# Attention inside a fused kernel: per-row maxima turned by VectorE instead of TensorE

## The chip, the cores and the metric

The kernel runs on one core of a Trainium2 chip. The metric is the device time of one execution in microseconds, and the figure compared is the median of several executions. Engines are named as the profile names them: PE is TensorE, DVE is VectorE, ACT is ScalarE, POOL is GpSimd and SP is SyncE, which here only issues transfers.

## What is computed

The kernel runs a causal attention with a decay, then two mixture-like matrix stages on its output. The change lies in the attention alone:

```python
# q, k, v: (4, 8, 576, 64); f: (4, 8, 576)
scores = scale * np.matmul(q, k.transpose(0, 1, 3, 2))
cum = np.cumsum(np.log(np.clip(f, 0.0001, 1.0)), axis=-1)
scores = np.where(causal, -1000000000.0, scores + cum[:, :, :, None] - cum[:, :, None, :])
scores = scores - np.max(scores, axis=-1, keepdims=True)
attn = np.exp(scores)
attn = attn / (np.sum(attn, axis=-1, keepdims=True) + 1e-09)
out = np.matmul(attn, v)
# then: x = out as (2304, 512); x = ((x @ w1) * (x @ w2)) @ w3 @ w_out
# then: every row goes to one of 8 experts (512 -> 1024 relu -> 512) and is gated
```

## The kernel before, in words

The attention works on 16 units, one for each of 4 batches and 4 pairs of heads. A unit's scores are computed twice. The first time queries lie on the partitions, so that a maximum over the keys is a reduction along the free axis. The second time keys lie on the partitions, so that the weights come out in the layout that the product with `v` needs. Between the two the maxima have to change from a column (one number per partition) into a row, since the second pass adds them by a product with one row of a matrix.

The steps of unit n, by the names in the table `START` (L50):

- `X1`, `X3`, `X2` (`scores_of`, L229) and `XL` (`scores_last`, L248) are the products of the first pass on PE. `XL` holds the last 64 queries of both heads. Their results lie in three PSUM buffers (`pss`, L94), which the eight tiles of a unit use in turn: a product waits until the reader of the tile three places before it is done.
- `m0` to `m3` and `mL` (`maxima`, L257, L262) are the reductions on DVE. Each writes one column of the tile `M` of the unit: columns 0 to 7 are the four blocks of 128 queries for each head, column 8 is the last block for both heads.
- `Tm` (`turn`, L268) is a PE transpose of `M` into a free corner of a score tile in PSUM. For units 2 to 14 that is the tile of `X1` of the next unit. `tc` (`turned`, L273) is an ACT copy of nine rows from there to the tile `mt` in SBUF. `mv` (`spread_maxima`, L276, issued through `move`, L193) is two SP transfers from `mt` into rows 0 and 64 of the tile `MR`.
- `GA` to `GD` are the second pass on PE, `HA` to `HD` (`weights`, L281, with `last`) add decay and maxima to it from `CK` and `MR`, and `eA` to `eD` (L301) are the exponentials on ACT, which write the tile `PT`.
- `a0` to `a4` (L307) and `s1` to `s3` (L319) are the causal masks of `PT` and the sums over its blocks on POOL.
- `p0`, `p1`, `p3` (L328) are the products with `v` on PE. They and the sums `su` (L344) belong to the unit before the one whose `PT` is being made.
- `kh`, `qh` (ACT, L213) and `kl`, `ql` (DVE, L220) split the operands into a high and a low part. `lk`, `lq`, `lv` (L198) are the loads of k, q and v on SP, `ck` (L207) is the load of the decay rows into `CK`, `qd` (L193) copies the last queries into `QD`, `zs` (L355) stores the sums of the weights.
- `c0` to `c6` convert one piece of a later weight per unit: `c0` is its load on SP (L465), `c1` and `c5` are ACT (L472, L481), `c2`, `c3`, `c4` are DVE (L474, L476, L478), `c6` is POOL (L483). `xm` (L380) is a further POOL product in units 5, 7, 9 and 11.

The order is written out by hand. Every step has a time `START[x] + SHIFT[n, x] + PERIOD * n`, all steps of all units are sorted by it, and every engine executes its own in that order. The times set the order on an engine and nothing else; waits come from data and from buffers in use. After the attention, and already among its last units, PE multiplies the converted weight pieces (`AFTER`, L64), and the matrix stages follow.

Of the kernel before, what the change touches and what calls it, by code (L numbers as in the profile page):

```python
# [11 lines left out]
F32 = mybir.dt.float32  # L12
F32R = mybir.dt.float32r
# [4 lines left out]
ACTF = mybir.ActivationFunctionType  # L18
# [4 lines left out]
B, H, S, D = 4, 8, 576, 64  # L23
NP = H // 2
# [4 lines left out]
P = 128  # L29
# [18 lines left out]

PERIOD = 9.8
START = {  # L50
# [8 lines left out]
}  # L59
SHIFT = {(0, "ck"): 8.38, (1, "ck"): 8.38, (2, "ck"): 8.38, (3, "ck"): 8.38, (0, "qd"): -2.0, (0, "lq"): 7.41, (0, "lk"): 14.91, (1, "lk"): 15.41, (2, "lk"): 14.9, (3, "lk"): 5.8, (4, "lk"): 2.1, (2, "lq"): 0.5, (0, "kh"): 5.05,  (1, "lq"): 0.5, (0, "XL"): -4.55, (0, "mL"): -5.9, (0, "Tm"): -1.8, (0, "tc"): -1.8, (0, "mv"): -2.6, (1, "Tm"): -0.1, (1, "tc"): -0.1}  # L60

FILL = {(0, "XL"): 10, (1, "X0"): 1, (0, "HA"): 1, (0, "HB"): 3, (1, "XL"): 3, (2, "X0"): 2}

# [13 lines left out]
def attention(nc, tc, ident, xT, rz, xs, wc, q, k, v, f):  # L77
# [6 lines left out]
    V, A, G, PE, SP = nc.vector, nc.scalar, nc.gpsimd, nc.tensor, nc.sync  # L84
    with (
# [31 lines left out]
        MRs = [p1.tile([P, S], F32R, name=f"MR{i}") for i in range(2)]  # L117
# [3 lines left out]
        Ms = [p1.tile([P, 64], F32, name=f"M{i}") for i in range(2)]  # L121
# [58 lines left out]
        st = {}  # L180

        def tl(s, key, shape, dt=F32, bufs=2):
            if key in ("kh", "kl"):
                ring = KHs[key == "kl"]
                s[key] = ring[s["n"] % len(ring)]
                return s[key][:, :S]
            if key not in s:
                pool = p2 if key in ("qr", "kr", "kh", "kl", "qh", "ql") else p3
                s[key] = pool.tile([P, *shape], dt, name=f"{key}_{s['n']}", tag=key, bufs=bufs)
            return s[key]  # L190

        def move(out, src):
            SP.dma_start(out=out.bitcast(F32), in_=src.bitcast(F32))  # L193
# [71 lines left out]
                    accum_out=Ms[s["n"] % 2][:, c:c + 1],  # L265
                )

        def turn(s):  # L268
            x = st[s["n"] + 1]["x", 1][:, 256:] if 1 < s["n"] < B * NP - 1 else s["x", 4][:, 896:]
            s["t"] = x[0:64, :P]  # L270
            PE.transpose(s["t"], Ms[s["n"] % 2], ident)

        def turned(s):  # L273
            A.activation(out=tl(s, "mt", (P,), F32R)[0:9], in_=s["t"][0:9], func=ACTF.Copy)

        def spread_maxima(s):  # L276
            t, MR = s["mt"], MRs[s["n"] % 2]
            move(MR[0:P:64, 0:512].rearrange("h (i c) -> h i c", c=P), t[0:8])
            move(MR[0:P:64, 512:S], t[8:9])

        def weights(s, g, last):  # L281

# [91 lines left out]
        def first_tile(s, x):  # L374
# [5 lines left out]
                    G.tensor_tensor(out=xT[:, i, 0:512], in0=xT[:, i, 0:512], in1=d, op=ALU.mult)  # L380

        stages = {
            "ck": (decay,), "qd": (last_queries,), "XL": (scores_last,), "mL": (maxima, 4), "Tm": (turn,), "tc": (turned,), "mv": (spread_maxima,),
            "p0": (pv, (0,)), "p1": (pv, (1, 2)), "p3": (pv, (3, 4)), "su": (sums,), "xa": (weighted,), "sa": (keep_sums,),
            "zs": (store_sums,), "rl": (invert, 0), "ra": (invert, 1), "rv": (invert, 2), "rs": (invert, 3), "xl": (first_tile, 0), "xm": (first_tile, 1),
        }
# [13 lines left out]
        for n in range(B * NP):  # L400
            st[n] = {"n": n}
        order = [(START[x] + SHIFT.get((n, x), 0.0) + PERIOD * n, n, i, x) for n in range(B * NP) for i, x in enumerate(START)]
        order = sorted(order + [(t + PERIOD * (B * NP - 1), B * NP, 0, x) for x, t in AFTER.items()])
# [864 lines left out]
def program(shapes):  # L1268
    nc = bacc.Bacc("TRN2", target_bir_lowering=False, num_devices=1)
    a = {n: nc.dram_tensor(n, s, mybir.dt.from_np(t), kind="ExternalInput").ap() for n, (s, t) in shapes.items()}  # L1270
    out = nc.dram_tensor("out", (N, DM), F32, kind="ExternalOutput").ap()
    with tile.TileContext(nc) as tc:
        with tc.tile_pool(name="keep", bufs=1) as keep, tc.tile_pool(name="raws", bufs=2, reuse_waits="tile") as raws, tc.tile_pool(name="div", bufs=1, space=DRAM) as div:
            rz = div.tile([NP, 2, N], F32, name="rz")

            xs = div.tile([E * N, DM + 2], F32, name="xs")
            ident = keep.tile([P, P], F32, name="ident")
            last = keep.tile([P, 64], F32, name="last")[:, :36]
            make_identity(nc, ident)
            xpool = ExitStack()  # L1280
            xt = xpool.enter_context(tc.tile_pool(name="xt", bufs=1, side="right"))
            xT = xt.tile([P, NP, N], F32, name="xT")
            region = ExitStack()
            region.enter_context(tc.manual_schedule())
            wc = Combined(nc, tc, xpool, raws, a["wo"], a["w3t"], last)
            attention(nc, tc, ident, xT, rz, xs, wc, a["q"], a["k"], a["v"], a["f"])
            moe(nc, tc, ident, xT, rz, xs, xpool, raws, region, wc, a["w1"], a["w2"], a["gates"], a["e1"], a["e2"], out)
            xpool.close()
    return nc
# [9 lines left out]
```

## Time and profile before

| | us |
|---|---|
| median of 3 runs (788.97 to 789.41) | 788.98 |
| the profiled execution | 790.18 |
| its span, first to last instruction | 788.5 |
| PE busy | 769.2 (98%) |
| DVE busy | 450.0 (57%) |
| ACT busy | 280.4 (36%) |
| POOL busy | 319.9 (41%) |

The attention fills about the first 175 us of the span. Its units follow each other at some 9.8 to 10.7 us, except for the first two and the last. The shares of the whole span say little about it: DVE and POOL are busy for most of the attention and for less than half of the rest.

### The profile page before, as it was taken

The page shows a single profiled execution, that of the slowest core. Times are in us where ns is not written, and L with a number is a line of the kernel's source. Part 1 is how long each engine was busy: PE and PEld are TensorE (multiplying, and loading weights), DVE is VectorE, ACT ScalarE, POOL GpSimd, SP SyncE. Part 2 cuts the span into 40 slices and gives each one's busy share as a digit, 9 for nine tenths or more (in the row PEclk, how much of TensorE's full clock was granted, in tenths as well). Part 3 has the DMA queues.
Part 4 walks back from the last instruction along what each step waited for, and adds up shares of the span by engine and source line. Part 5 has one row for each costly group of instructions (what it writes and reads, how often), then busy time and mean ns, then how long its engine had stood idle before and what let it go on. Part 6 is the DMA issues. An engine that isn't in the chain of part 4 may idle for free. (4 is left out here: it accounts for less than half of the span.)

```text
span 788.5 us, 13727 instructions
## 1 busy us (share of the span) xinstructions
PE 769.2 (98%) x5126; PEld 637.5 (81%) x5126; DVE 450.0 (57%) x983; ACT 280.4 (36%) x542; POOL 319.9 (41%) x343
## 2 busy tenths in 40 slices
PE   8999999999999999999999999999999999999995
PEld 4677766677888877887887888898797999999983
DVE  7789999979799604233250422347468645545620
ACT  3566666655475122212212221314221222322221
POOL 6689999990000401130230111134444544455420
PEclk9999999999999999999999999999999999999998
DMA  3555555445543191010100000054677556456460
GB/s 105 180 153 161 153 159 159 121 131 166 183 161 131 37 349 47 28 40 14 55 20 1 34 28 0 18 169 137 214 235 227 151 205 224 138 188 215 145 267 30
DMA packets 40211, 102.12 MB, mean 130 GB/s; under 512 B 8610, under 2 KB 9314, under 8 KB 39888
## 3 DMA queue, kind: packets, MB, share of 16 engines
q1 hardware_dynamic: 36960, 91.46, 36.4%
q0 software_dynamic: 3184, 9.77, 3.3%
q8 instruction: 41, 0.67, 0.3%
q14 instruction: 26, 0.21, 0.1%
HBM read 84.47 MB, written 16.51 MB: 128 GB/s over the span
## 5 line engine op out<-in xcount | busy, mean ns | idle before, releaser
L598 DVE TENSOR_TENSOR ga<-b,ga 128x512 f32<-128x512 f32 (+1 forms) x40 | 25.4, 635 | 127.2 <-PE b L570 126.5
L729 POOL DMA_INDIRECT xs<-xr,pos x18 | 19.8, 1101 | 173.2 <-DVE pos L723 127.5
L262 DVE CUSTOM_DVE_ANT_0 junk<-x,tri 128x256 f32<-128x256 f32 (+3 forms) x128 | 62.7, 490 | 14.2 <-PE x L227 3.6
L568 PE MATMUL h<-gh,ah 128*128 128x320 f32 (+4 forms) x224 | 67.2, 300 | 0.0
L569 PE MATMUL h<-gl,ah 128*128 128x320 f32 (+4 forms) x224 | 66.9, 299 | 0.0
L570 PE MATMUL h<-gh,al 128*128 128x320 f32 (+4 forms) x224 | 66.9, 299 | 0.0
L568 PE MATMUL b<-xh,w2h 128*128 128x512 f32 (+1 forms) x160 | 60.0, 375 | 0.0
L568 PE MATMUL a<-xh,w1h 128*128 128x512 f32 (+1 forms) x160 | 59.8, 374 | 0.0
L570 PE MATMUL a<-xh,w1l 128*128 128x512 f32 (+1 forms) x160 | 58.9, 368 | 0.0
L570 PE MATMUL b<-xh,w2l 128*128 128x512 f32 (+1 forms) x160 | 58.9, 368 | 0.0
L569 PE MATMUL a<-xl,w1h 128*128 128x512 f32 (+1 forms) x160 | 58.9, 368 | 0.0
L569 PE MATMUL b<-xl,w2h 128*128 128x512 f32 (+1 forms) x160 | 58.8, 368 | 0.0
L568 PE MATMUL y<-raw,gh 128*128 128x512 f32 x144 | 56.8, 395 | 0.0
L600 ACT ACTIVATE gh<-ga 128x512 fp32r<-128x512 f32 (+1 forms) x40 | 23.5, 589 | 93.1 <-DVE ga L598 93.1
L570 PE MATMUL y<-raw,gl 128*128 128x512 f32 x144 | 56.2, 390 | 0.0
L569 PE MATMUL y<-raw,gh 128*128 128x512 f32 x144 | 56.1, 389 | 0.0
L561 POOL TENSOR_SCALAR bh<-rb 128x1024 fp32r<-128x1024 f32 x28 | 37.3, 1334 | 45.9 <-DMA rb<-e 42.6
L307 POOL TENSOR_SCALAR_AFFINE_SELECT PT<-PT 128x256 f32<-128x256 f32 (+1 forms) x80 | 47.2, 613 | 18.0 <-ACT PT L301 17.7
L1025 DVE SCALAR_TENSOR_TENSOR hl<-h,hh 128x320 fp32r<-128x320 f32 (+4 forms) x56 | 25.5, 462 | 46.9 <-ACT hh L1024 46.3
L584 POOL TENSOR_TENSOR xT<-xT,rz 128x512 f32<-128x512 f32 (+1 forms) x16 | 19.8, 1237 | 77.3 <-ACT w2h L481 77.3
L328 PE MATMUL v<-PT,vr 128*64 128x448 f32 (+4 forms) x384 | 49.8, 396 | 0.0
L319 POOL TENSOR_TENSOR ac<-ac,PT 128x640 f32<-128x640 f32 (+1 forms) x32 | 45.3, 1415 | 1.7
(617 smaller groups left out, 2109.2 us busy)
## 6 DMA issues: line engine op xcount, KB each, us to landing
ra<-e SPq DMA_DIRECT2D x28, 512.0 KB
rb<-e SPq DMA_DIRECT2D x28, 512.0 KB
w<-w3t SPq DMA_DIRECT2D x16, 512.0 KB
xs<-zero SPq DMA_DIRECT2D x8, 771.0 KB
vr<-v SPq DMA_DIRECT2D x16, 320.0 KB
kr<-k SPq DMA_DIRECT2D x16, 288.0 KB
qr<-q SPq DMA_DIRECT2D x16, 288.0 KB
wo<-wo SPq DMA_DIRECT2D x8, 512.0 KB
```

The costliest lines, as they stand in the source:

```text
L262: V.tensor_tensor_reduce(out=junk[:, :w], in0=s["x", i][:, 512 * h:512 * h + w] if i < 4 else s["x", i][:, 224:224 + S], in1=tri[:, 640 - ...
L307: G.affine_select(out=t, in_=t, pattern=[[0, 2], [1, w]], compare_op=ALU.is_ge, fill=0.0, base=0, channel_multiplier=-1,)
L319: G.tensor_tensor(out=acc[:, :, q0 - P:], in0=first if j == 1 else acc[:, :, q0 - P:], in1=src, op=ALU.add)
L328: PE.matmul(s["v"][HALF[h], 384 + q0:384 + q1], s["vr"][:, j, HALF[h]], place(s, j, h, q0, q1), start=(j == 0), stop=(j == 4 or q1 == P),)
L561: G.tensor_scalar(out=hi, in0=src, scalar1=1.0, scalar2=1.0, op0=ALU.mult, op1=ALU.mult)
L568: PE.matmul(ps, ah, bh, start=start and i == 0, stop=False)
L569: PE.matmul(ps, ah, bl, start=False, stop=False)
L570: PE.matmul(ps, al, bh, start=False, stop=stop and i == last)
L584: G.tensor_tensor(out=xv, in0=xv, in1=d, op=ALU.mult)
L598: V.tensor_tensor(out=ga[:, :w], in0=pb[:, :w], in1=ga[:, :w], op=ALU.mult)
L600: A.activation(out=gh[:, f, :w], in_=ga[:, :w], func=ACTF.Copy)
L1025: V.scalar_tensor_tensor(out=hl[:, f, :w], in0=ps[:, :w], scalar=0.0, in1=hh[:, f, :w].bitcast(F32), op0=ALU.max, op1=ALU.subtract)
```

## The change

`Tm` becomes a DVE transpose of the first 32 columns of `M` in blocks of 32 by 32 straight into `mt` in SBUF; PE and ACT have no part in it any more. It stands right after `m0`, that is before `mL` of the same unit, and turns columns 0 to 7 only. Each of the four blocks of 32 partitions then goes into the row by a transfer of its own (eight pieces of 32 numbers). In unit 0 two of the four are issued by ACT, all others by SP. Column 8 is not turned: the new step `ml` moves it after `mL`, straight from the column, number by number, into its place in the row. So a unit has five transfers where it had two, in other places of SP's order: `mv` moves from behind `qd` to behind `lk`, and `ml` stands ahead of `lq`, `zs` and `lv`, whose times are moved a little to come behind it. The decay rows `ck` of units 2 and 3 go earlier.

```diff
-    ... "lq": -16.9, ...
+    ... "lq": -15.95, ...
-    "kl": 1.21, "XL": 2.1, "mL": 3.54, "Tm": 4.8, "tc": 4.85, "ql": 1.3, "mv": 5.7, "GA": 8.35,
+    "kl": 1.21, "XL": 2.1, "mL": 3.54, "Tm": -1.2, "ml": 3.56, "ql": 1.3, "mv": -1.15, "GA": 8.35,
-    ... "lv": 13.2, ... "zs": 32.77, ...
+    ... "lv": 13.55, ... "zs": 33.1, ...
-SHIFT = {..., (2, "ck"): 8.38, (3, "ck"): 8.38, ..., (0, "lq"): 7.41, ..., (0, "Tm"): -1.8, (0, "tc"): -1.8, (0, "mv"): -2.6, ...}
+SHIFT = {..., (2, "ck"): 5.9, (3, "ck"): 4.3, ..., (0, "lq"): 6.46, ..., (0, "mv"): 4.2, (0, "ml"): -0.45}
-        def turn(s):
-            x = st[s["n"] + 1]["x", 1][:, 256:] if 1 < s["n"] < B * NP - 1 else s["x", 4][:, 896:]
-            s["t"] = x[0:64, :P]
-            PE.transpose(s["t"], Ms[s["n"] % 2], ident)
-
         def turned(s):
-            A.activation(out=tl(s, "mt", (P,), F32R)[0:9], in_=s["t"][0:9], func=ACTF.Copy)
+            V.transpose(out=tl(s, "mt", (32,)), in_=Ms[s["n"] % 2][:, :32])

         def spread_maxima(s):
-            t, MR = s["mt"], MRs[s["n"] % 2]
-            move(MR[0:P:64, 0:512].rearrange("h (i c) -> h i c", c=P), t[0:8])
-            move(MR[0:P:64, 512:S], t[8:9])
+            MR = MRs[s["n"] % 2].bitcast(F32)
+            for b in range(4):
+                (A if s["n"] == 0 and b > 1 else SP).dma_start(
+                    out=MR[0:P:64, 0:512].rearrange("h (i b k) -> h i b k", b=4, k=32)[:, :, b], in_=s["mt"][32 * b:32 * b + 8],
+                )
+
+        def spread_last(s):
+            SP.dma_start(out=MRs[s["n"] % 2][0:P:64, 512:S].bitcast(F32), in_=Ms[s["n"] % 2][:, 8:9])
```

## Rows read from the trace of the kernel before

**Rows 1.** Stretches: us, then busy us of each engine, TensorE clock, DMA share, GB/s

```profile
39.00:98.00 59.00, 58.74 (x666) 43.38 (x664) 53.01 (x142) 40.34 (x69) 52.43 (x54) 1.00 0.53 155
98.00:160.00 62.00, 59.83 (x668) 43.18 (x666) 58.31 (x139) 40.22 (x68) 60.70 (x58) 1.00 0.48 145
160.00:290.00 130.00, 130.00 (x703) 104.83 (x700) 98.37 (x164) 61.66 (x109) 28.39 (x32) 1.00 0.48 162
290.00:788.50 498.50, 486.88 (x2842) 425.67 (x2840) 211.79 (x440) 120.70 (x272) 152.51 (x160) 1.00 0.35 115
```

**Rows 2.** Timeline of PE, middle of a unit: start, us, operation [idle before]

```profile
83.99 0.45 PE L227 MATMUL x<-CK,OQ 64*128 64x384 f32 x4
84.48 0.30 PE L271 MATMUL x<-ident,M 128*64 128x128 f32 x1
84.70 1.95 PE L328 MATMUL v<-PT,vr 128*64 128x448 f32 x16
```

**Rows 3.** Timeline of DVE and POOL, `kl` and what stands beside it

```profile
39.44 0.75 DVE L220 TENSOR_TENSOR kl<-kr,kh 128x576 fp32r<-128x576 f32 x1
...
78.63 1.57 DVE L220 TENSOR_TENSOR kl<-kr,kh 128x576 fp32r<-128x576 f32 x1
...
78.38 1.20 POOL L319 TENSOR_TENSOR ac<-ac,PT 128x384 f32<-128x384 f32 x1
79.96 1.39 POOL L307 TENSOR_SCALAR_AFFINE_SELECT PT<-PT 128x256 f32<-128x256 f32 x2 [0.38 <-ACT PT L301]
```

**Rows 4.** Timeline of POOL, the first sum `s1` of six units

```profile
43.22 2.11 POOL L319 TENSOR_TENSOR ac<-PT 128x896 f32<-128x896 f32 x1
...
53.27 2.11 POOL L319 TENSOR_TENSOR ac<-PT 128x896 f32<-128x896 f32 x1
...
82.83 2.12 POOL L319 TENSOR_TENSOR ac<-PT 128x896 f32<-128x896 f32 x1
...
92.62 2.11 POOL L319 TENSOR_TENSOR ac<-PT 128x896 f32<-128x896 f32 x1
...
124.38 2.10 POOL L319 TENSOR_TENSOR ac<-PT 128x896 f32<-128x896 f32 x1
...
134.11 2.09 POOL L319 TENSOR_TENSOR ac<-PT 128x896 f32<-128x896 f32 x1
```

**Rows 5.** Groups of DVE by shape: count, busy us, mean ns, idle before

```profile
L262 DVE DVE_READ_ACCUMULATOR2_ANT M<- 128x1 f32 x144 | 11.8, 82 | 0.0
L370 DVE RECIPROCAL z<-z 128x36 f32<-128x36 f32 x3 | 1.1, 372 | 0.0
```

**Rows 6.** Timeline of PE, `GC` of unit 0

```profile
21.42 0.50 PE L227 MATMUL gC<-qh,kh 64*128 64x448 f32 x4 [0.85 <-DVE M L262]
```

**Rows 7.** Timeline of PE and POOL, the turn of unit 14 and the attention's end

```profile
154.87 0.45 PE L227 MATMUL x<-CK,OQ 64*128 64x384 f32 x4
155.81 1.95 PE L328 MATMUL v<-PT,vr 128*64 128x448 f32 x16
...
175.49 3.23 POOL L319 TENSOR_TENSOR ac<-ac,PT 128x640 f32<-128x640 f32 x2
...
179.54 0.44 PE L344 MATMUL v<-ac,ones 128*32 128x288 f32 x2
```

**Rows 8.** SP's issues, the products that use them, transfers into `MR`, the wait for them

```profile
80.23 0.33 SPq L198 DMA_DIRECT2D kr<-k  x1
83.41 1.17 SPq L193 DMA_DIRECT2D QD<-qh  x2
...
81.09 0.40 PE L254 MATMUL xl<-kh,QD 128*128 128x288 f32 x1
88.14 0.41 PE L227 MATMUL gA<-MR,CK 64*128 64x192 f32 x4
...
L193 SPq DMA_DIRECT2D MR<-mt x32: 512/554/580, 15.9 to 165.1; - x32
PE gA L227 <- DMA MR<-mt: 0.2, 1, 0.2
```

More of the change, by code (lines that the diff above doesn't have):

```diff
@@ L50 @@
 START = {
[1 row of a table removed]
[1 row of a table added]
     "X1": -5.99, "m1": -5.27, "X3": -5.12, "X2": -5.07, "m3": -2.49, "X0": -1.58, "m2": -1.5, "m0": -1.24, "qd": -4.8,
[1 row of a table removed]
[1 row of a table added]
     "HA": 8.43, "GB": 8.46, "HB": 8.5, "GC": 8.77, "HC": 9.64, "eA": 10.17, "eB": 10.24, "eC": 11.25, "GD": 11.28,
[1 row of a table removed]
[1 row of a table added]
     "s1": 13.9, "a2": 14.0, "s2": 14.5, "c6": 17.0, "s3": 17.5, "p0": 22.91, "p1": 24.73,
[1 row of a table removed]
[1 row of a table added]
     "rs": 48.4,
 }
-SHIFT = {(0, "ck"): 8.38, (1, "ck"): 8.38, (2, "ck"): 8.38, (3, "ck"): 8.38, (0, "qd"): -2.0, (0, "lq"): 7.41, (0, "lk"): 14.91, (1, "lk"): 15.41, (2, "lk"): 14.9, (3, "lk"): 5.8, (4, "lk"): 2.1, (2, "lq"): 0.5, (0, "kh"): 5.05,  (1, "lq"): 0.5, (0, "XL"): -4.55, (0, "mL"): -5.9, (0, "Tm"): -1.8, (0, "tc"): -1.8, (0, "mv"): -2.6, (1, "Tm"): -0.1, (1, "tc"): -0.1}
+SHIFT = {(0, "ck"): 8.38, (1, "ck"): 8.38, (2, "ck"): 5.9, (3, "ck"): 4.3, (0, "qd"): -2.0, (0, "lq"): 6.46, (0, "lk"): 14.91, (1, "lk"): 15.41, (2, "lk"): 14.9, (3, "lk"): 5.8, (4, "lk"): 2.1, (2, "lq"): -0.45, (0, "kh"): 5.05,  (1, "lq"): -0.45, (0, "XL"): -4.55, (0, "mL"): -5.9, (0, "mv"): 4.2, (0, "ml"): -0.45}
 FILL = {(0, "XL"): 10, (1, "X0"): 1, (0, "HA"): 1, (0, "HB"): 3, (1, "XL"): 3, (2, "X0"): 2}
@@ L382, in attention @@
         stages = {
-            "ck": (decay,), "qd": (last_queries,), "XL": (scores_last,), "mL": (maxima, 4), "Tm": (turn,), "tc": (turned,), "mv": (spread_maxima,),
+            "ck": (decay,), "qd": (last_queries,), "XL": (scores_last,), "mL": (maxima, 4), "Tm": (turned,), "mv": (spread_maxima,), "ml": (spread_last,),
             "p0": (pv, (0,)), "p1": (pv, (1, 2)), "p3": (pv, (3, 4)), "su": (sums,), "xa": (weighted,), "sa": (keep_sums,),
```

6 rows, old and new, of the table START are left out of this document.

## The prediction

> **What bounds the kernel now.** I read the stretches first, then the timelines of PE, DVE and POOL over single units, then the waits. From 160 to 290 us PE is busy for the whole 130.00 us, and afterwards it idles 11.6 us in 498.5 [rows 1]. So the attention's end is handed on almost one for one: what PE's stream gains or loses by 180 us or so, the kernel gains or loses. The question is what sets the pace until then, and the stretches give two answers. From 39 to 98 us PE has nearly no idle time (58.74 of 59). From 98 to 160 us it has 2.2 us, and POOL is busy for 60.70 of 62 [rows 1].
>
> The rows on `kl` show how POOL and DVE hang together. This subtraction takes 0.75 us at 39.44 and 1.57 us at 78.63, where the sum `s3` on POOL starts at 78.38 and takes 1.20 [rows 3]. 78.38 + 1.20 = 79.58, and `kl` ends at 80.20, about 0.6 later: it did nearly all its work after `s3` had ended. The masks behind it take 1.39 for two, while DVE runs `ql` and the weight conversions. So POOL and the DVE instructions with two SBUF operands run in turn, and POOL's round plus DVE's share makes a cycle of its own. The start of `s1` from unit to unit measures it. From 124.38 to 134.11, in the stretch where PE waits, it is 9.73 us, and that is what the cycle needs by itself. From 82.83 to 92.62, where PE is full, it is 9.79 [rows 4]. PE and this cycle therefore have nearly the same pace, and taking work from one of them alone uncovers the other. POOL's wait for ACT ahead of the masks, 0.38 at 79.96 [rows 3], looks like slack, but for most of it DVE holds the turn (`kl` until 80.20).
>
> [...]
>
> **The PE turn, removed.** In the middle of a unit the last score product starts at 83.99. Its like take about 0.23 until the next one starts, so PE is free at 84.22; the turn starts at 84.48 and the next product at 84.70 [rows 2]. A turn costs PE 0.48 us, half of it waiting for DVE. Sixteen of them are 7.7 us of PE time. How much is on the path depends on the stretch:
> - From 39 to 98 us the cycle of POOL and DVE takes over as soon as PE is quicker. The gain is at most 9.79 - 9.73 = 0.06 per unit, in some five units 0.3. The first two of these units had 10.05 from `s1` to `s1` (43.22 to 53.27 [rows 4]), because POOL came late to a cycle that was waiting for PE; these can close towards 9.73, 0.6 in all at best. Bounds for the whole stretch are 0 and 0.9 gained; I take 0.3, since POOL is nearly full already.
> - From 98 to 160 us PE waits anyway, and removing a turn moves the wait to the next product. I take 0.
> - At the end PE is the pace again. The turn of unit 14 lies between 154.87 + 0.22 and 155.81 [rows 7], which is 0.72; that of unit 15 costs at least the 0.22 from a turn's start to the next product [rows 2]. Together they give 0.94. But the sums of unit 15 start at 179.54 and need POOL's last sum, which ends at 175.49 + 3.23 = 178.72 [rows 7]. So at most 0.82 can be gained before POOL is late next. I take 0.77, a little being lost to signalling; the lower bound is 0.22.
>
> **The ACT copy, removed.** ACT is busy for 40 of 59 us [rows 1] and waited for the turn itself. I take 0; nothing behind it was late.
>
> **The DVE turn, added.** No row shows one. The cheapest DVE instruction on the same tile, the reading of the accumulator, takes 82 ns, and a short two-sided one, the reciprocal of 128x36, takes 372 ns [rows 5]. With some 0.1 us between dependent instructions the step costs DVE 0.15 to 0.45; I take 0.2, nearer to the first, since 32 columns are few.
> - Unit 0: DVE works through from its first maximum, and PE's `GC` waits 0.85 for it at 21.42 [rows 6]. The turn of unit 0 stands ahead of that: 0.2 lost, with bounds 0 and 0.45.
> - Units 1 and 2: DVE still waits for PE there, as `kl` at 39.44 without any blocking also says. 0.
> - From unit 3 to the end, the step stands between `m0` and `c2`, ahead of `kl`, and `kl` then waits up to 1.57 - 0.75 = 0.82 for POOL [rows 3]. That wait hides it, as long as `c2` doesn't miss its turn before `s3`. If the cover is gone, the price is 0.2 for each of some 12 units. I take 0.2 in all, with 0 and 2.4 as bounds; the upper one is a rival below.
>
> **The transfers.** A transfer into `MR` holds SP for 0.55 us [rows 8], so three more per unit are 1.7 us of SP. `mv` is now queued behind the load of k, which SP issues at 80.23 after waiting for `kl`: four transfers until 82.8, then `ck`. Then `ml` waits for `mL`, which ends about when `QD` is issued today, and behind `ml` are queued `lq`, `zs`, `lv`, `qd` and `c0`. `QD`, issued at 83.41, goes to about 85.4, and is needed by the next unit's `XL`, at about 81.09 + 9.79 = 90.88 [rows 4, 8]. q and v are needed nearly ten us after their issue, so two us later costs 0. A row that lands sooner gains 0 too: PE has waited for it once, for 0.2 us [rows 8]. How long 128 single numbers take to land no row shows. The nearest are the two transfers of today, which nearly always land in time. `ml` is issued from about 83.5 on and needed by `HA` at 88.14 [rows 8], so it has over 4 us; between 0 and a loss I take 0.
>
> [...]
>
> **The sum.** -0.77 at the end, -0.3 in the middle, +0.2 in unit 0, +0.2 later: -0.67 us. The profiled execution, 790.18 (span 788.5 and 1.7 around it), would become 789.5. The median of the runs is 1.2 below the profiled one, so 788.98 becomes 788.3. This case by itself reaches from 787.4 (the middle at 0.9) to 789.8 (the end at 0.22, the turn at 0.45 in unit 0, and half its later cover gone).
>
> **The rivals.**
> - PE alone bounds the middle. For it: PE is full there, and POOL shows a wait for ACT in every unit. Against it: 9.73 per unit in the stretch where PE has time to wait. Then 0.48 for each of seven units (2 to 8), 3.4, is gained, less 0.2, and 0.77 at the end: -3.9, or 785.1.
> - DVE becomes the bound. Its place is the step between `m0` and `kl`. DVE is busy for 53 of 59 us, and in the saturated units it goes from `kl` to `mL` without a wait for PE. If the step makes `c2` miss its turn before `s3`, each of 12 units is later by the step's whole cost. It decides from a cost of about 0.25 on: 12 x 0.25 = 3.0, + 0.25, - 0.77 = +2.4, or 791.4.
> - The row is late. If `ml` needs more than 4 us to land, `HA` waits in every unit; 1 us of it costs some 13 us. The transfers shown speak against it. About 800.
> - The change doesn't do what it says for the time: the row comes sooner, but nobody waited for it. That is part of my forecast, in which the gain comes from PE's missing turn.
>
> **How the numbers follow.** The forecast has 0.60, PE as the bound 0.20, DVE as the bound 0.15, the late row 0.05. A measurement can tell about 0.2%, 1.6 us, from no change, so the edges are 787.4 and 790.6. Of the forecast 0.03 fall below and 0.02 above, and of DVE as the bound 0.03 falls within: faster 0.23, same 0.58, slower 0.19. The range goes from 785.6 to 791.0: it takes in the bounds of the unknown costs and the near parts of the first two rivals.
>
> **What would show it.** After the change, PE's idle time from 39 to 98 us should grow by about 0.4 per unit, in front of the second product of a unit or of `GC`, with DVE as the releaser; the spacing of `s1` should stay near 9.75. The product with `v` should follow the score products at once. The DVE turn should take 0.08 to 0.37 us. `kl` should be shortened by about what the turn takes. The end of the attention (the sums of unit 15) should come 0.5 to 1 us sooner. The prediction is wrong if the spacing of `s1` falls below 9.6 (first rival) or rises above 9.9 (second), or if PE waits for `MR`.

## The result, and the profile after

| | before | after |
|---|---|---|
| median of 8 runs each, us | 789.50 (788.97 to 790.41) | 794.04 (791.23 to 795.02) |
| the profiled execution, us | 790.18 | 795.02 |
| its span, us | 788.5 | 793.4 |

The changed kernel is slower: 1.0052 times the time before, with a 95% interval from 1.0044 to 1.0061. That is 4.1 us (4.5 between the medians); the prediction had 788.3 and a range from 785.6 to 791.0.

The stretches of the profile after, for [rows 1], with two more at the start (columns as there):

```profile
10.00:20.00 10.00, 7.71 (x58) 4.74 (x55) 8.66 (x30) 2.21 (x4) 3.55 (x6) 0.94 0.45 129
20.00:30.00 10.00, 9.76 (x52) 6.54 (x54) 4.03 (x14) 4.90 (x7) 4.07 (x7) 0.55 0.43 126
39.00:98.00 59.00, 58.52 (x660) 42.52 (x658) 54.30 (x149) 38.60 (x62) 55.71 (x54) 1.00 0.57 155
98.00:160.00 62.00, 56.33 (x638) 41.07 (x636) 58.18 (x138) 37.03 (x58) 58.71 (x55) 1.00 0.53 150
160.00:290.00 130.00, 129.16 (x738) 103.64 (x735) 104.92 (x184) 62.34 (x109) 34.97 (x38) 1.00 0.45 148
```

The second of these stretches in the kernel before:

```profile
20.00:30.00 10.00, 8.44 (x77) 5.69 (x75) 7.14 (x27) 4.38 (x8) 6.25 (x8) 1.00 0.61 191
```

Three things stand out. From 20 to 30 us PE is busy, and yet its granted clock is 0.55; before it was 1.00 there. From 39 to 98 us POOL has gone from 52.43 to 55.71 us while PE hardly changed. From 98 to 160 us PE is busy for 3.5 us less than before, and POOL for 2 us less: both wait for something.

What PE does ahead of the drop (timeline of PE after: start, us, operation [idle before and what ended it]):

```profile
15.30 0.50 PE L227 MATMUL x<-kh,qh 64*128 64x384 f32 x4 [0.37 <-DVE M L262]
16.02 0.39 PE L171 MATMUL fill<-warm 128*128 128x512 bf16 x1
17.67 0.51 PE L227 MATMUL gA<-qh,kh 64*128 64x192 f32 x4 [1.25 <-DVE M L262]
18.98 0.82 PE L227 MATMUL gA<-MR,CK 64*128 64x192 f32 x4 [0.32 <-DMA MR<-mt]
```

The same place in the kernel before:

```profile
15.29 0.30 PE L271 MATMUL xl<-ident,M 128*64 128x128 f32 x1 [1.41 <-DVE M L262]
...
17.44 0.51 PE L227 MATMUL gA<-qh,kh 64*128 64x192 f32 x4
```

Before, PE waited for the maxima ahead of its turn of unit 0 and did the products of unit 1 behind it. Without the turn the products are done sooner, one filler product follows (a product of the tile `warm` that nobody reads), and then PE idles for 1.25 us ahead of `gA` of unit 0. The length of the idle time doesn't tell the two kernels apart: before, PE idled for 1.41 us ahead of its turn, and the clock stayed at 1.00.

What POOL and PE wait for later. POOL's timeline after, the two `xm` that wait:

```profile
108.36 1.28 POOL L380 TENSOR_TENSOR xT<-xT,rb 128x512 f32<-128x512 f32 x1 [2.24 <-DMA rb<-rz]
...
150.29 1.30 POOL L380 TENSOR_TENSOR xT<-xT,rb 128x512 f32<-128x512 f32 x1 [0.55 <-DMA rb<-rz]
```

The tile `rb` is loaded by the step `xl` (`first_tile`, on SP through `spread`, L74). SP's queue after, in the unit of the first of these loads:

```profile
93.68 0.33 SPq L198 DMA_DIRECT2D kr<-k  x1
94.06 2.27 SPq L274 DMA_DIRECT2D MR<-mt  x4
96.38 0.62 SPq L372 DMA_DIRECT2D rz<-z  x1
97.10 0.73 SPq L207 DMA_DIRECT2D CK<-EKd  x2
97.93 0.55 SPq L279 DMA_DIRECT2D MR<-M  x1
98.53 0.46 SPq L198 DMA_DIRECT2D qr<-q  x1
99.09 0.51 SPq L355 DMA_DIRECT2D zd<-zs  x1
99.65 0.40 SPq L198 DMA_DIRECT2D vr<-v  x1
100.15 1.16 SPq L193 DMA_DIRECT2D QD<-qh  x2
101.37 0.57 SPq L465 DMA_DIRECT2D w<-w3t  x1
101.98 1.10 SPq L74 DMA_DIRECT2D rb<-rz  x2
```

and the same load in the kernel before, with the `xm` that uses it and doesn't wait:

```profile
90.01 0.33 SPq L198 DMA_DIRECT2D kr<-k  x1
...
96.61 1.14 SPq L74 DMA_DIRECT2D rb<-rz  x2
...
102.38 1.29 POOL L380 TENSOR_TENSOR xT<-xT,rb 128x512 f32<-128x512 f32 x1
```

SP has no gap of more than 0.1 us from 93.68 to 103.08. The load of `rb` is its last issue in the unit and goes out 5.4 us later than before, while the attention as a whole is only some 3 us later there. From the load of k (`kr`) to that of `rb` it takes 6.60 us before and 8.30 after: 1.7 us more, as much as three transfers. The load lands after POOL has come to `xm`.

The lag of the changed kernel, read at `eA`, builds up as these two places say: 1.1 us at unit 0, 2.7 at unit 1, 3.6 at unit 2, 3.1 at unit 9, 4.5 at unit 10, 5.5 at unit 15. At the end of the span it is 4.9. The 1.1 at unit 0 is for the most part not the clock's: 0.8 of it stands in the first kernel below, too, where the clock doesn't fall (19.56 against 18.73).

### The profile page after: what moved, and what is told of

Read it like the earlier page. It is cut to its first block, busy times and chain, and to the rows that moved or that the text cites. A ratio compares the mean times of both kernels' runs of the same rounds, so it can differ in the third digit from the quotient of the medians.

```text
span 793.4 us, 13773 instructions
## 1 busy us (share of the span) xinstructions
PE 769.6 (97%) x5108; PEld 638.0 (80%) x5110; DVE 453.6 (57%) x999; ACT 276.1 (35%) x526; POOL 320.8 (40%) x343
## 4 chain that ended last, share of the span: by engine, by line
PE 72%; DVE 11%; POOL 6%; issue 5%; DMA 3%; ACT 0%; SPq 0%; ACTq 0%; DVEq 0%; POOLq 0%
DVE junk L262 6%; PE a L568 4%; PE b L568 4%; PE y L570 4%; PE y L568 4%; PE y L569 4%; PE a L570 4%; PE b L570 4%; PE a L569 4%; PE b L569 4%; PE h L568 3%; PE h L570 3%; PE h L569 3%; POOL ac L319 3%; PE q L568 2%
## 5 line engine op out<-in xcount | busy, mean ns | idle before, releaser
L307 POOL TENSOR_SCALAR_AFFINE_SELECT PT<-PT 128x256 f32<-128x256 f32 (+1 forms) x80 | 49.3, 640 | 18.4 <-ACT PT L301 18.1
L561 POOL TENSOR_SCALAR bh<-rb 128x1024 fp32r<-128x1024 f32 x28 | 35.7, 1276 | 46.6 <-DMA rb<-e 41.0
```

Source lines behind the costliest of these rows:

```text
L307: G.affine_select(out=t, in_=t, pattern=[[0, 2], [1, w]], compare_op=ALU.is_ge, fill=0.0, base=0, channel_multiplier=-1,)
L561: G.tensor_scalar(out=hi, in0=src, scalar1=1.0, scalar2=1.0, op0=ALU.mult, op1=ALU.mult)
```

## The experiments

Two causes were suspected, PE's clock in the first units and the late load of `rb`. The first three kernels take them away one by one and together; the fourth brings PE's turn back. They ran beside 29 runs of the kernel before with a median of 791.06, which is 1.6 above the 789.50 of the result. So a kernel is compared with the runs of before that ran beside it: behind each time stands the ratio to them, with its 95% interval.

**Filler products in unit 1.**

```diff
-FILL = {(0, "XL"): 10, (1, "X0"): 1, ...
+FILL = {(0, "XL"): 10, (1, "X0"): 7, ...
```

> The changed kernel with six more filler products for TensorE between the score product X2 of unit 1 and the first weight product gA of unit 0, where TensorE now idles from about 16.0 to 17.7 us. Nothing is left out. Theory (the idle time in which the transposition stood cost the clock): the granted clock stays at 1.00 from 18 to 29 us where the changed kernel shows 0.50, the exponential eA of unit 3 starts some 3.3 us sooner than the 52.9 us there, and the time falls from 794.0 to about 790.7. The wait for the row of reciprocals at unit 8 stays (about 2.2 us). Rival (the loss of the first three units is VectorE's transposition and the transfers of unit 0): the time stays within 0.5 of 794.0 although the clock is full.

Measured 796.06 (794.40 to 796.83), 1.0057 [1.0044, 1.0070]: no gain over the changed kernel's 1.0052. The trace shows that the first part came as expected: the clock is 1.00 from 10 to 110 us, and `eA` of unit 3 starts at 49.18 instead of 52.91. But the wait for `rb` remained, the clock fell to 0.83 behind it, from 110 to 120 us, and once more past 300 us (0.83 from 300 to 310 us).

**The load of `rb` sooner.**

```diff
-    ... "xl": 36.3, ...
+    ... "xl": 34.8, ...
```

> The changed kernel with the load of the reciprocals' row (stage xl, broadcast into rb) moved 1.5 us sooner in the planned order, right behind the queries' transfer qd and ahead of the weight load of c0 on SP's queue. Nothing is left out. Theory (SP's longer queue makes that load late): the multiplication xm of unit 8 no longer waits for rb (2.24 us there in the changed kernel) and the time falls from 794.0 by some 2.2 to about 791.8; the clock still falls to 0.50 from 19 to 29 us. Rival (the lag past unit 9 is VectorE's transposition in units that VectorE bounds): the wait goes and the time stays within 0.5 of 794.0.

Measured 792.39 (790.43 to 794.49), 1.0013 [1.0002, 1.0024]. The wait at `xm` is gone, and with it 3.1 of the 4.1 us, by the ratios. In the profiled execution a part of that is the clock's: it falls less than in the first profile after (0.83 from 19 to 29 us, where that has 0.50), and `eA` of unit 1 starts at 29.76 instead of 32.40.

**Both.**

> The changed kernel with both edits: the six filler products in unit 1 and the load of rb ahead of c0's weight load. Nothing is left out. Theory (those two are the whole loss, and what the removed transposition gives at the end, some 0.6 us, remains): 794.0 - 3.3 - 2.2 = 788.5, with before at 789.5, so 788.0 to 789.5. Rival (the new way of turning costs by itself, in VectorE or in SP's queue): 790.5 or more.

Measured 791.94 (790.85 to 793.92), 1.0009 [0.9999, 1.0020], so 0.9 above before in the median and not below it, as the theory had it; the interval takes in no difference. The rival's 790.5 was set against a before of 789.5, so the time doesn't choose between the two.

**Both, with PE's turn as well.**

```diff
+        def turn(s):
+            x = st[s["n"] + 1]["x", 1][:, 256:] if 1 < s["n"] < B * NP - 1 else s["x", 4][:, 896:]
+            PE.transpose(x[0:64, :P], Ms[s["n"] % 2], ident)
```

> The kernel with both edits and, at its old place in every unit, TensorE's transposition of the maxima again, whose product nobody reads; the maxima still go the new way. Nothing of the computation is left out. It prices TensorE's transposition alone. Theory (hidden behind GpSimd's sums in the middle, worth 0.3 to 0.8 at the end): 0.3 to 1.2 us slower than the kernel with both edits. Rival (TensorE alone bounds the middle, so that each of some nine units gains 0.35 to 0.48): 3 us slower or more.

Measured 790.45 (789.55 to 791.87), 0.9996 [0.9987, 1.0004]: 1.5 us faster than without the extra work, which no theory had. Within attention the trace says the contrary: the last sums of PE start at 180.43 with the turn and at 179.31 without. So the difference had to lie behind attention. It lies at 297 us, where VectorE copies token numbers into a tile that is still being read by a store of zeroed rows. The copy's wait and what PE then waits for, before:

```profile
296.66 0.21 DVE L726 COPY xr<-tof 128x1 f32<-128x1 f32 x2 [21.22 <-DMA rz<-rz]
...
298.69 0.66 PE L678 MATMUL lg<-ident,lp 128*128 128x128 f32 x4 [0.74 <-ACT lp L675]
```

and with both edits, without PE's turn:

```profile
297.71 0.21 DVE L726 COPY xr<-tof 128x1 f32<-128x1 f32 x2 [22.48 <-DMA rz<-rz]
...
299.74 0.66 PE L678 MATMUL lg<-ident,lp 128*128 128x128 f32 x4 [2.00 <-ACT lp L675]
```

The releaser's name is inferred; the packets in flight are those of the store, 3072 of 2056 B. From its first packet to its last the store took 20.2 us before, 19.5 after, 21.6, 20.9 and 21.5 in the first three experiments and 19.1 in the fourth, and PE's wait followed it: 0.74, 0, 2.18, 1.41, 2.00 and 0. No run shows why its length differs.

To take this out, one line behind attention was edited so that the copy also reads `z` and VectorE reaches it only after the routing:

```diff
-                V.tensor_copy(xr[:, DM + 1:DM + 2], tof[:, c0 + c:c0 + c + 1])
+                V.scalar_tensor_tensor(out=xr[:, DM + 1:DM + 2], in0=z[:, c:c + 1], scalar=0.0, in1=tof[:, c0 + c:c0 + c + 1], op0=ALU.mult, op1=ALU.add)
```

All further kernels have it. The first four of them ran beside 27 runs of before (791.28), the other four beside 35 (791.23).

**The kernel before with that edit.**

> The kernel before with one edit behind attention: the copy of the token numbers into the rows (line 726) reads z too, as z times 0 plus the number, so that VectorE reaches it only after the routing and no longer stands from 275 to 297 us until the store of the zeroed rows has landed. Nothing is left out; the result is the same. Theory (that store, 19.1 to 21.6 us long in the six traces, holds TensorE 0 to 2.2 us at its transposition of lp at 299 us and so adds to every kernel a time that has nothing to do with the change): the wait of 0.74 us at 298.69 is gone, the time is 0.5 to 1.5 below before and its spread narrower. Rival (the store's landing is waited for by the next engine anyway): the same time as before.

Measured 788.91 (788.40 to 789.67), 0.9968 [0.9958, 0.9977]. It gives 2.4 us, more than expected, and the spread shrinks from 3.9 us to 1.3. It has the lowest median of all kernels tried here. The two profiled executions differ by 1.4 us (spans 788.5 and 787.1), of which 0.74 is the wait; no trace shows where the rest of the 2.4 lies. PE no longer waits at that place:

```profile
297.63 0.60 PE L678 MATMUL lg<-ident,lp 128*128 128x128 f32 x4
```

**The changed kernel with that edit.**

> The changed kernel with the same edit behind attention. Nothing is left out. Theory (the loss of 4 to 5 us arises within attention, before 175 us): 4 to 5.5 us over the kernel before with that edit. Rival (a good part of the loss arises behind attention, from the store): under 3 us over it.

Measured 792.38 (791.35 to 794.68), 1.0021 [1.0010, 1.0031]. That is 3.5 us over the kernel before with the same edit: below what was expected, but nearly the whole loss does arise within attention: PE's last sums start at 182.76 against 179.38.

**Both edits and that edit.**

> The changed kernel with the filler products in unit 1, the load of rb ahead of c0's weight load, and the same edit behind attention. Nothing is left out. Theory (with the two causes removed what the transposition gave TensorE at the end, 0.6 to 0.7 us, remains; the 0.7 us by which the kernel with both edits stood above before came from the store): 0.2 to 1.0 us below the kernel before with that edit, and below before and the changed kernel. Rival (the new way of turning itself costs something): 0.3 us or more above it.

Measured 789.31 (788.79 to 790.11), 0.9979 [0.9970, 0.9989]. It stands 0.4 us above the kernel before with the edit, and the two intervals overlap: no difference that can be told, where 0.2 to 1.0 below was expected. It is 2 us faster than before and 3.1 faster than the changed kernel with the edit, so the two causes together are nearly the whole loss. POOL's longer busy time from 39 to 98 us was no part of it: it is 55.95 us here, as against 55.71 in the changed kernel.

**The late load alone, in the kernel before.**

```diff
-    ... "xl": 36.3, ...
+    ... "xl": 38.5, ...
```

> The kernel before with the edit behind attention and with the load of rb (stage xl) 2.2 us later in the planned order, so that it stands behind the next load of kr on SP's queue (issued at about 100.1 us instead of 96.6); the maxima are turned by TensorE as before. Nothing is left out. Theory (a late rb alone makes GpSimd wait at xm and so delays everything behind it): GpSimd waits 2 to 3 us for rb at 102 us and the time rises by 1 to 3 us over the kernel before with the edit behind attention. Rival (GpSimd has that much slack at that place, and the loss of the changed kernel had another cause): within 0.5 us of it.

Measured 793.59 (793.33 to 794.64), 1.0033 [1.0020, 1.0045], 4.7 us over its base and more than expected. Its SP, POOL and PE at that place:

```profile
100.01 1.16 SPq L74 DMA_DIRECT2D rb<-rz  x2
...
105.08 1.28 POOL L380 TENSOR_TENSOR xT<-xT,rb 128x512 f32<-128x512 f32 x1 [2.83 <-DMA rb<-rz]
...
115.45 0.50 PE L227 MATMUL x<-kh,qh 64*128 64x384 f32 x4 [2.21 <-DVE M L262]
```

and the stretch behind it, in this kernel and then in its base:

```profile
110.00:120.00 10.00, 7.48 (x53) 4.07 (x49) 9.36 (x22) 4.08 (x7) 9.92 (x11) 0.86 0.42 108
```

```profile
110.00:120.00 10.00, 9.39 (x105) 6.48 (x105) 9.36 (x23) 6.24 (x11) 9.81 (x11) 1.00 0.57 162
```

A load that goes out 3.4 us later makes POOL wait 2.83 us. The wait reaches PE one unit later as 2.21 us of idle time, and then the clock falls too. From `eA` of unit 9 to that of unit 10 it takes 14.14 us instead of 10.60, and a second `xm` waits 1.7 us. The maxima are turned the old way here, so the late load needs no help from the rest of the change. What of the 4.7 us is the clock's, which is 1.00 there in the base, isn't told apart; from 10 to 20 us, ahead of the late load, it is 0.83 here, too, and 1.00 in the base.

**Each cause alone.**

> The changed kernel with the six filler products in unit 1 and the edit behind attention; the load of rb stays where the change leaves it. Nothing is left out. Theory (the wait for rb sits at the same place of the pipeline however early attention's first units are, and TensorE's clock may fall behind it): GpSimd waits about 2.2 us at xm and the time is 3 to 4.5 above the kernel before with the edit behind attention, so 792 to 793.5. Rival (the falling clock of the first units is worth a part of its own that the filler gives back): 791.4 or less.

Measured 791.90 (790.17 to 792.95), 1.0005 [0.9992, 1.0018]: 2.6 over the kernel with both edits in the median, 2.1 by the ratios (1.0005 against 0.9979), which is the late load alone. In the median it is 3.0 over the kernel before with the edit, where the theory had 3 to 4.5. POOL waits 1.91 us at `xm` at 104.46; the clock stays at 1.00 behind it, from 110 to 120 us, and the span is 2.2 us longer (789.3 against 787.1).

> The changed kernel with the load of rb ahead of c0's weight load and the edit behind attention, without the filler products. Nothing is left out. What it stands above the kernel with both edits (789.3) is the price of the clock that falls in the first units. Theory: 0.3 to 1.5 us, so 789.6 to 790.8, with the granted clock under 1.00 between 19 and 29 us. Rival (the clock's price of 3.3 us that the first profile of the changed kernel showed holds in most executions): 792 or more.

Measured 791.14 (788.95 to 793.98), 0.9995 [0.9981, 1.0008]: 1.8 over the kernel with both edits in the median, 1.3 by the ratios: in the median more than expected and less than the rival had. This kernel spreads over 5 us, from the time of the kernel with both edits up: its fastest execution has a mean granted clock of 0.997, its slowest 0.990. In the profiled one, at 792.36, the clock falls as in the first profile after. Its stretch from 19 to 29 us, with PE's wait ahead of it and `eA` of unit 1:

```profile
17.66 0.51 PE L227 MATMUL gA<-qh,kh 64*128 64x192 f32 x4 [1.26 <-DVE M L262]
...
19.00:29.00 10.00, 9.76 (x46) 6.37 (x47) 4.20 (x15) 4.86 (x7) 3.15 (x5) 0.50 0.49 154
...
32.47 0.97 ACT L301 ACTIVATE PT<-gA 128x960 f32<-128x960 f32 x1 [3.27 <-PE gA L227]
```

and in the kernel with both edits, where filler products stand in place of that wait:

```profile
19.00:29.00 10.00, 9.23 (x85) 6.72 (x89) 6.87 (x24) 5.10 (x8) 5.43 (x7) 1.00 0.67 196
...
28.85 0.97 ACT L301 ACTIVATE PT<-gA 128x960 f32<-128x960 f32 x1 [2.39 <-PE gA L227]
```

With the clock at 0.50 PE is busy for 9.76 of the ten us, and gets through 46 products there where the kernel with both edits gets through 85. Where the clock is 0.50 for these ten us, `eA` of unit 1 comes 3.6 us later (32.47 - 28.85), and that stays to the end: the spans are 790.7 and 787.1.

All four profiled executions without the six filler products show a fall at this place, but not of one size. Here and in the first profile after, the clock is 0.50 over these ten us; in the changed kernel with the edit behind attention it is

```profile
19.00:29.00 10.00, 9.71 (x72) 6.25 (x75) 5.95 (x22) 4.94 (x7) 4.41 (x7) 0.83 0.59 176
```

and 0.83 likewise with the load of `rb` sooner alone. In these two `eA` of unit 1 starts at 29.73 and 29.76, 0.9 to 1.1 us later than with the products. All seven with the products have 1.00 from 20 to 30 us, and six of them from 10 to 20 us as well; the one with VectorE's turn twice, the last kernel below, has 0.83 from 10 to 20. So with the filler products no profile shows the fall that runs past 20 us. Why it is 0.50 in one execution and 0.83 in another no run shows. By the medians the two prices, 2.6 and 1.8, add up to more than the 3.1 that both causes cost at once; by the ratios they are 2.1 and 1.3, and both at once 3.3. So it isn't shown that the two overlap.

**The price of PE's turn.** (the kernel with both edits, with PE's turn as above)

> The kernel with both edits and the edit behind attention, and TensorE's transposition of the maxima again at its old place in every unit, its product read by nobody; the maxima go the new way. Nothing of the computation is left out. Theory (it lies beside GpSimd's sums in most units and on the path at the end): 0.3 to 1.2 us above the kernel with both edits, so 789.6 to 790.5, and TensorE reaches the last sums (v, line 344) about 1 us later. Rival (TensorE alone bounds the middle): 3 us or more. Rival (it is hidden everywhere): within 0.2.

Measured 789.70 (789.09 to 790.49), 0.9974 [0.9963, 0.9985]: in the median 0.4 over the kernel without it, by the ratios 0.4 under it, and the intervals overlap. So the time rules out the 3 us of the first rival and can't choose between the theory and the second. The traces can tell more. PE's product with `v` in the middle and its last sums, without the turn:

```profile
84.06 1.95 PE L328 MATMUL v<-PT,vr 128*64 128x448 f32 x16
...
179.21 0.44 PE L344 MATMUL v<-ac,ones 128*32 128x288 f32 x2 [0.32 <-POOL ac L319]
```

and with it:

```profile
85.07 1.24 PE L332 MATMUL v<-PT,vr 128*64 128x448 f32 x6
...
180.21 0.44 PE L348 MATMUL v<-ac,ones 128*32 128x288 f32 x2
```

The turn costs 1.00 us by 84 us, some 0.35 at each of three turns: the product with `v` behind them starts at 36.18, 45.93 and 55.69 instead of 35.80, 45.21 and 54.63. From there to 155 us it costs nothing (the difference stays at about 1.00 in each unit). At the end it adds 0.39 again (169.45 and 170.84), and without it PE waits 0.32 us for POOL's last sum, which takes that back. Of the 1.00 us at the last sums, 0.5 is left at the end of the span (787.6 against 787.1); no run shows where the other half goes.

**The price of VectorE's turn.**

```diff
+            V.transpose(out=tl(s, "mu", (32,)), in_=Ms[s["n"] % 2][:, :32])
```

> The kernel with both edits and the edit behind attention, and VectorE's transposition of the maxima done twice in every unit, the second into a tile that nobody reads. Nothing of the computation is left out. It prices that instruction, 211 ns each in the trace. Theory (hidden behind the instructions of GpSimd that VectorE takes turns with, on the path only in units 0 to 3 and at the end): 0 to 0.6 us above the kernel with both edits. Rival (VectorE bounds the units from the fourth on, where a unit takes 9.81 us against 9.76 before): 0.2 us in each of some twelve units, 2 us or more.

Measured 789.59 (788.91 to 791.09), 0.9977 [0.9967, 0.9988]: in the median 0.3 over the kernel with one turn, by the ratios 0.2 under it. That is no difference that can be told, and the rival's 2 us are ruled out. Its VectorE in a middle unit:

```profile
89.47 0.21 DVE L269 STREAM_TRANSPOSE mt<-M 128x32 f32<-128x32 f32 x1
89.61 0.17 DVE L270 STREAM_TRANSPOSE mu<-M 128x32 f32<-128x32 f32 x1
89.70 0.76 DVE L475 TENSOR_SCALAR wo3u<-wo3u 128x512 int32<-128x512 int32 x1
90.39 0.74 DVE L220 TENSOR_TENSOR kl<-kr,kh 128x576 fp32r<-128x576 f32 x1
```

The wait for POOL has moved from `kl` (1.57 in [rows 3] and with one turn, 0.74 here) to the conversion ahead of it (0.76, where it takes 0.38 with one turn; it ends at 90.46, and `s3` on POOL at 90.18), and hides most of the second turn too. Three units from one sum `s1` to another take 9.85 us each here (64.20 to 93.75, with single ones from 9.29 to 10.36), 9.81 with one turn (63.12 to 92.56) and 9.76 in the kernel before with the edit (63.22 to 92.49).

## Why the prediction was wrong

- **The transfers: "q and v are needed nearly ten us after their issue, so two us later costs 0."** This is the step that failed. The count was right: 1.6 us more of SP, at 0.52 us a transfer, where 1.7 was predicted. So was the list of what stands behind `ml`, as far as it went: `lq`, `zs`, `lv`, `qd`, `c0`. It stopped one short. Behind `c0`, in units 5, 7, 9 and 11, stands `xl`, whose load is used by `xm`, and `xm` stands in POOL's order ahead of the sum `s1`. The rows that were read are from a unit without it. By itself that late load costs 2.1 to 2.6 us, and 4.7 in the kernel before, where the sum had 0. A `QD` that is late once by 0.8 us in the same stretch (PE's `xl` at 114.39) is issued from the same queue.
- **The PE turn, removed, in unit 0.** The prediction priced PE's half microsecond and what PE could do with it. It didn't ask what becomes of the idle time in which the turn stood: the products of unit 1 move ahead, the idle time gathers ahead of `gA`, and PE's granted clock falls to 0.50. The sum has no term for this. It costs 3.6 us where the clock is 0.50 over the ten us from 19 to 29, 0.9 to 1.1 where it is 0.83 over them, and over the runs 1.8 by the medians, 1.3 by the ratios. The 0.2 us that the prediction put on unit 0 for VectorE is small beside it: with the gap filled, `eA` of unit 0 starts 0.8 later than in the kernel before (19.54 against 18.74, both with the edit behind attention), and `eA` of unit 1 0.9 sooner (28.85 against 29.76), so nothing of it is left.
- **The PE turn, removed, elsewhere.** 0.3 us in the middle and 0.77 at the end were predicted. The traces show about 0.7 between 39 and 98 us, within the bounds of 0 and 0.9, another 0.35 just ahead of that stretch, at 36 us, where the prediction had no term, and none at the end. There POOL's last sum is late next, as the prediction said it would be from 0.82 on; it is so at once, because POOL itself comes to that sum later (it ends at 179.15 with both edits, at 178.55 in the kernel before, both with the edit behind attention). That the sum of both terms, 1.07, comes out is luck: two errors cancel. No gain from 98 to 160 us is right.
- **The DVE turn.** 0.15 to 0.45 us were bounds and 0.2 was taken. The 0.1 us between dependent instructions stood in no row; the trace of before has it at 300.51 us, where the comparison that reads a maximum starts 0.22 us after it (at 300.73), and the independent sum between them 0.11 after it. The instruction takes 0.21:

```profile
L269 DVE STREAM_TRANSPOSE mt<-M 128x32 f32<-128x32 f32 x16 | 3.4, 212 | 0.6
```

  The cover is there, but not where the prediction had it: `kl` isn't shortened, it takes 1.57 with both edits as before; the conversion ahead of it is, from 0.58 to 0.38 us. That conversion reads one tile only, and yet it took 0.76 us beside `s3` with the second turn: in these traces not only the instructions with two operands take longer beside POOL's. And it isn't whole. Where PE waits, the cycle of POOL and DVE takes 9.73 us in the kernel before and 9.81 with both edits (134.23 - 124.42); from 39 to 98 us it is 9.81 against 9.76. From unit 5 to unit 14 the lead of the kernel with both edits, read at `eA`, shrinks from 0.76 to 0.19 us. So the units behind the first ones lose some 0.6 us, where 0.2 was taken with bounds of 0 and 2.4. That the turn itself is what lengthens them isn't shown: a second one adds only 0.04 a unit.
- **The late row.** `ml` was given a small chance to be late, and a wait of PE for `MR` was a sign of being wrong. PE waited for the row once in the whole attention, ahead of the last product of `gA` of unit 0, 0.50 us with the load of its weights and 0.32 with the product:

```profile
18.95 0.53 PEld L227 LDWEIGHTS gA<-MR,CK 64*128 64x128 f32 x4 [0.50 <-DMA MR<-M]
18.98 0.82 PE L227 MATMUL gA<-MR,CK 64*128 64x192 f32 x4 [0.32 <-DMA MR<-mt]
```

  The kernel with both edits has the same wait and loses nothing that can be told. Apart from that one wait, PE waits for no transfer into `MR` in the trace of the changed kernel.
- **"The attention's end is handed on almost one for one."** True once the store is out of the way: from the last sums to the end of the span it takes 607.7 us in the kernel before, 607.6 in the changed one and 607.9 with both edits, and 607.4 to 608.2 in all eight kernels with that edit. Without that edit PE's wait at 299 us adds 0 to 2.2 us of its own. The prediction saw the 11.6 us of idle time and didn't look at what ended them.
- **The sum.** -0.67 is added up rightly. The two ends of the forecast's own reach are not: the middle at 0.9 gives 787.7 and not 787.4, and the terms named for the other end give 790.1 and not 789.8. Neither changes the range. The base, 788.98, was the median of three runs; that of eight is 789.50.
- **The signs.** From 39 to 98 us the spacing of `s1` stayed between 9.7 and 9.9 us, the turn took what was said, and the product with `v` did follow the score products. PE's idle time from 39 to 98 us grew by 0.2 us in all (0.26 to 0.48; 0.79 with both edits), not by 0.4 in each unit. And the last sums of unit 15 came only 0.2 us sooner even with both causes removed (179.21 against 179.38), not 0.5 to 1.
- **The rivals.** None of them came. PE alone as the bound would have given 3 us or more for the turn, DVE as the bound 2 us or more for a second one. The slower side had been given to DVE and to the row; it came from SP's queue.

With the two causes removed the change is worth nothing that can be told. In the traces PE's missing turn gives 1.0 us up to the last sums, and all but 0.2 of that is lost again, to the longer units and at the end.

## What to carry to other kernels

When transfers are added to a queue, list what is behind them to the end of the period, in every kind of unit, and follow each to its reader and to what stands behind the reader on that engine. When work is taken from PE, ask where the idle time gathers that it had divided. And before a difference of a few tenths per cent is explained, look for a wait far behind the change whose length varies from run to run: here one line took it out and was worth more than the change could have been.

## What was not expected of the hardware

- PE's granted clock fell at 19 us after PE had idled 1.25 us, and 0.32 us a little later, although PE was busy for over 9.7 of the ten us that followed. Over these ten us it was 0.50 in two profiled executions and 0.83 in two others with the same instructions up to there. In all seven in which filler products stood in the 1.25 us it was 1.00 from 20 to 30 us, and in one of them 0.83 from 10 to 20. In the kernel before, PE idled 1.41 us at 15.29 and it stayed at 1.00 from 10 to 30 us; with the late load, which comes at 100 us, it was 0.83 from 10 to 20.
- VectorE's transposition of 128x32 numbers takes 211 ns, and 169 ns where another stands right ahead of it.
- A store of 3072 packets of 2056 B took between 19.1 and 21.6 us in six executions.
